# A gated-recurrence layer feeding a cosine-gated MLP in fp32: the start of the kernel reordered, the seven products taken in another order, and the quarter sums of w_out made earlier

## The chip, the cores and the metric

The kernel runs on one core of one Trainium2 chip. The metric is the device time of one execution in microseconds. The kernel before took 660.46 us (the median of three runs: 659.95, 660.46 and 667.34).

## The reference, cut to what matters

Inputs `q, k, v, a_re, a_im` have the shape (B=4, H=8, S=768, D=48); `w_in` is 384 x 2048 and `w_out` 2048 x 384, both in double precision, so that the kernel must turn their 64-bit words into fp32.

```python
mag = np.sqrt(a_re*a_re + a_im*a_im)
scale = np.minimum(mag, 0.999) / (mag + 1e-06)
a_re_n, a_im_n = a_re*scale, a_im*scale
for t in range(S):
    S_re, S_im = (ar*S_re - ai*S_im + k[t] (x) v[t],  ar*S_im + ai*S_re)
    y[t] = q[t] @ S_re
x = y.transpose(0, 2, 1, 3).reshape(B*S, H*D)     # 3072 x 384
h = x @ w_in
out = (h * np.cos(h)) @ w_out                     # 3072 x 384
```

The recurrence is a complex decay for each head and each key dimension; its product over time can be written as exp of a sum of logarithms times a cosine or sine of a sum of angles.

## The kernel before, in words

**Tiling.** The 768 steps of each batch are cut into chunks of 128, which makes 24 chunks (`n`), and two chunks make a group (`g`), 12 groups in all. For a group, the function `log_steps` makes log magnitude and tangent of the half angle from `a_re` and `a_im` on ScalarE and VectorE; for group 0 it runs separately for each of the two halves (`i` = 0, 1; the two generators are called `one` and `two`), each half 128 x 384 elements. `p_powers` sums the logarithms over the steps with a matmul against a triangle of ones (`lgs`, constant tile `sums`) and takes exp of plus and minus the sum (`P`, `Q`). `even_steps` refines them on VectorE. `g_angle` takes the arctangent, `g_phase` sums the angles with another triangle (`phs`, constant tiles `turns` and `last`), `g_trig` takes sine and cosine. `p_apply` and `g_stack` multiply keys and queries by them (`ks`, `qs`), each then of width 96. For groups 0 and 1 TensorE transposes them (`tp`, with `ident`); from group 2 on VectorE's block transpose and a round trip through DRAM does it (`moved`, L922 to L928).

**The chunk.** `f_scores` makes scores (`sc`) and VectorE masks them with `causal` (`atm`); `f_rows` or `f_out` multiplies them by the values and adds queries times the state carried from the chunk before (`yr`, `yp`); `state_sums` and `state_next` carry the state. The state must be multiplied by the decay over the whole chunk: the last row of `P`, moved from one partition to 96 by way of DRAM. `even_steps` issues these DMAs on SyncE's queue: `row` (L828), and, when that has landed, two `end` (L831). VectorE scales `end` in `p_end` (L839) and uses it in `state_next`.

**The MLP.** `mm1_sums` makes h in pieces `hp` (eight for a group), `gate_sine` and `gate_product` make h cos h. For groups 0 and 1 `mm2` multiplies by `w_out` directly (`op`). From group 2 on (`PLAIN`), each pair of chunks is a 2 x 2 block product done as seven products of half size instead of eight (`seventh`, L1150), with sums of blocks on the left (`mixed`, tiles `s`) and on the right (`quarters` and `last_quarter`, tiles `t_s1`, `t_s2`, `t_a22`, and `w_out`'s upper right block overwritten). Four of the seven add into one bank of PSUM that is never cleared between them (`sum`: products 0, 3, 5, 6), three have banks of their own (`op`: 1, 2, 4). ScalarE copies a scaled running sum out (`scalar.mul` into `ot`), VectorE adds an `op` product to it.

**Order.** Each engine runs its instructions in program order. Up to L1543 the order on TensorE, VectorE and ScalarE is written out by hand (L1292 to L1542): groups 0 and 1 with the conversion of the weights, a `piece` being one VectorE step of a weight tile, `lows` the ScalarE step, and 16 raw tiles of 768 KB fetched on GpSimd's queue through four buffers. After that the loop at L1548 weaves for each group n the chunks of n, the MLP products of n-1 and the preparation of n+1, each part given a stretch of the iteration (0 to 1); a scheduler then orders the engines' queues, with some orders fixed by hand (`behind`).

**The start.** SyncE's queue issues the loads of group 0 (`re`, `im` of both halves, then `k`, `q`, then `v`) and of group 1. `constant` (L534) puts a constant's load on ScalarE's queue, and six of them (L575 to L580) stand in the program ahead of ScalarE's first activation table (L1293). GpSimd waits for the second half of `im` by copying one element (`wait_for`, L1283) before it fetches raw weights. `busy(n)` issues n matmuls on a tile of ones, whose results are not used, to keep TensorE occupied.

Of the kernel before, what the change touches and what calls it, by code (L numbers as in the profile page):

```python
# [487 lines left out]
def fast_path(ctx, tc, q, k, v, a_re, a_im, moe_w_in, moe_w_out, out, least, odd, wide,  # L488
# [7 lines left out]
    nc = tc.nc  # L496
# [37 lines left out]
    def constant(array, name, queue=nc.scalar, pool=consts):  # L534
        t = pool.tile(list(array.shape), F32, name=name)
        queue.dma_start(out=t, in_=nc.inline_tensor(array, name=name + "_const").ap())
        return t
# [37 lines left out]
    ident = constant(np.eye(C, dtype=np.float32), "ident", pool=stage["pool"])  # L575
    upto = [constant(sums_np[0], "sums", pool=stage["pool"])]
    turns = [constant(sums_np[0] * np.float32(1.0 / math.pi), "turns", pool=stage["pool"])]
    last = constant(last_np, "last", pool=stage["pool"])
    carry = constant(carry_np, "carry")
    causal = constant(causal_np * np.float32(0.25), "causal")  # L580
# [70 lines left out]

    late = {}
    tail = {}

    def chain(ins, engine="scalar"):

        if engine in tail:
            behind(ins, tail[engine])
        tail[engine] = ins

    def behind(ins, other):
        tc.add_manual_dep(ins.ins, other.ins.name, mybir.DependencyInfo(
            mybir.DependencyClass.NoSync, mybir.DependencyReason.DATA))
# [71 lines left out]
    def log_steps(g, i, n):  # L735
# [10 lines left out]
        chain(nc.scalar.activation(out=m2, in_=re, func=AF.Square))  # L746
        chain(nc.scalar.activation(out=sq, in_=im, func=AF.Square))
# [62 lines left out]
    def even_steps(g, i, n):  # L810


        x = X[g]
        u = cut(x["mag"], i, n)
        P, Q = cut(x["P"], i, n), cut(x["Q"], i, n)
        ins = [vector.scalar_tensor_tensor(out=u, in0=Q, scalar=HUGE, in1=P,
                                           op0=ALU.min, op1=ALU.mult)]
        yield
        for t in P, Q:
            ins.append(vector.scalar_tensor_tensor(out=t, in0=u, scalar=3.0, in1=t,  # L820
                                                   op0=ALU.subtract, op1=ALU.mult))
            yield

        for one_, what in zip(ins, ("carried", "split")):
            if what in x and g > PEG:
                behind(one_, x[what])
        row = x["row"][ds(i * DM, n * DM)]
        nc.sync.dma_start(out=row, in_=P[C - 1:C].rearrange("o x -> (o x)"))  # L828
        end = x["end"][:, ds(i * H, n * H)]
        for a in range(2):  # L830
            nc.sync.dma_start(out=end[ds(a * D, D)], in_=row.rearrange("(x d) -> d x", d=D))  # L831
# [280 lines left out]
    def quarters():  # L1112

        for name in "s1", "s2", "a22":
            right[name] = stage["pool"].tile([C, HJ, E2], F32, name="t_" + name)
        t1, t2, t4 = (right[name] for name in ("s1", "s2", "a22"))
        for j in range(0, HJ, 2):
            for t, a, b in (t1, b12, b11), (t2, b22, t1), (t4, b21, t2):
                yield lambda t=t, a=a, b=b, j=j: behind(vector.tensor_tensor(
                    out=t[:, ds(j, 2)], in0=a[:, ds(j, 2)], in1=b[:, ds(j, 2)],  # L1120
                    op=ALU.subtract), Y[PLAIN * G]["masked"])
# [28 lines left out]
    def seventh(g, p, part):  # L1150
# [19 lines left out]
        if p in (0, 2, 5) or p == 6 and not alone:  # L1170
            late["scalar"] = scalar.mul(out={0: c11, 2: c21, 5: c22, 6: c12}[p], in_=ps, mul=scale)
        if g == NG - 1 and p == 5:
            scalar.mul(out=c12, in_=ps, mul=scale)
        if p in (1, 3, 4, 5) or alone:
            part_ = {1: c11, 3: c21, 4: c21, 5: c22, 6: c12}[p]
            added = vector.scalar_tensor_tensor(out=part_, in0=x["op"] if p == 5 else ps, scalar=scale,
                                                in1=part_, op0=ALU.mult, op1=ALU.add)
            if alone:
                behind(added, late["read DVE"])
            late["vector"] = added  # L1180
# [3 lines left out]
        elif p == 5:  # L1184
# [105 lines left out]
    pieces = [weight(dst, src) for dst, src in parts[:RAW]]  # L1290
# [365 lines left out]
```

## Time and profile before

| | us |
|---|---|
| runs | 659.95, 660.46, 667.34 |
| profiled execution, its own time | 667.46 |
| its span | 665.7 |
| TensorE busy | 650.7 (98%) |
| VectorE busy | 490.6 (74%) |
| ScalarE busy | 393.5 (59%) |
| GpSimd busy | 27.9 (4%) |
| mean granted TensorE clock | 0.988 |

The span runs from the first to the last instruction in the profile; 1.76 us of the execution's own time lie outside it. PE is TensorE's matmuls, PEld its weight loads, DVE is VectorE, ACT ScalarE, POOL GpSimd, SP SyncE; SPq, ACTq and POOLq are the DMA issues of these queues. A line such as `DVE atm L679 [7.87 <-PE sc L690]` says that VectorE stood idle for 7.87 us ahead of this instruction and that the matmuls `sc` ended the wait. Many operations go through a helper that records them all, so that L679 (VectorE and ScalarE), L690 (matmuls) and L710 (activations from a table) say little, and the tile's name says what it is. PEclk is the share of TensorE's full clock that was granted.

### The profile page before, as it was taken

What the parts mean: (1) busy time and instruction counts of PE and PEld (TensorE: products, weight loads), DVE (VectorE), ACT (ScalarE), POOL (GpSimd) and SP (SyncE); (2) the same over time, 40 slices, a digit from 0 to 9 for tenths busy, and PEclk for the clock granted to TensorE, in tenths of its full rate; (3) what the DMA queues carried; (4) which work ended last, traced back from release to release, by engine and by line L of the source; (5) the groups of instructions that cost most, each with busy time, mean ns of one, the idle gap of its engine ahead of it and who ended that gap; (6) DMA issues with size and microseconds to landing.
All of it is one profiled execution on the core that took longest, in us unless ns stands there. A gap on an engine that the chain in (4) does not pass through costs nothing.

```text
span 665.7 us, 10771 instructions
## 1 busy us (share of the span) xinstructions
PE 650.7 (98%) x4077; PEld 582.8 (88%) x4077; DVE 490.6 (74%) x797; ACT 393.5 (59%) x728; POOL 27.9 (4%) x47
## 2 busy tenths in 40 slices
PE   8899999999999999999999999999999999999996
PEld 6797977776899899899899899999999989999896
DVE  4977989869886887876877867876877868862251
ACT  6848696475484485485485485476476476432230
POOL 2011010000000010000000000000000000000000
PEclk9969999999999999999999999999999999999999
DMA  9946684727816827836837746846846853363001
GB/s 242 209 153 149 169 289 77 187 68 148 208 28 130 220 81 159 202 106 152 217 100 162 201 109 135 225 115 132 227 118 132 225 120 96 119 142 96 25 1 31
DMA packets 233626, 94.90 MB, mean 143 GB/s; under 512 B 208846, under 2 KB 222033, under 8 KB 233564
## 3 DMA queue, kind: packets, MB, share of 16 engines
q1 hardware_dynamic: 226924, 68.52, 45.1%
q0 software_dynamic: 5632, 25.17, 11.3%
q8 instruction: 34, 0.56, 0.4%
q10 hardware_dynamic: 1008, 0.43, 0.3%
q14 instruction: 28, 0.23, 0.1%
HBM read 69.28 MB, written 24.81 MB: 141 GB/s over the span
## 4 chain that ended last, share of the span: by engine, by line
PE 79%; DMA 7%; DVE 6%; ACT 2%; SPq 2%; issue 2%; POOL 0%; DVEq 0%; POOLq 0%
PE hp L690 31%; PE op L690 17%; PE sum L690 13%; PE sc L690 5%; PE yp L690 5%; PE sp L690 3%; PE phs L690 2%; DMA qT<-moved 2%; SPq L925 2%; PE lgs L690 1%; DMA raw<-in_moe_w_out_dram 1%; DMA xT<-x 1%; DVE mag L679 1%; PE yr L690 1%; DVE qs L679 1%
## 5 line engine op out<-in xcount | busy, mean ns | idle before, releaser
L690 PE MATMUL hp<-xT,w_in 128*128 128x256 f32 (+1 forms) x1176 | 255.3, 378 | 0.9 <-DMA xT<-x 0.9
L690 PEld LDWEIGHTS hp<-xT,w_in 128*128 128x128 f32 x1176 | 222.2, 193 | 31.9 <-DMA xT<-x 1.4
L710 ACT ACTIVATE gate<-hp,half_pi_b 128x512 f32<-128x512 f32 x96 | 66.0, 687 | 119.5 <-PE hp L690 119.5
L679 DVE TENSOR_TENSOR gate<-hp,gate 128x512 f32<-128x512 f32 x96 | 65.5, 682 | 48.2 <-ACT junk L679 48.1
L690 PE MATMUL op<-w_out,gate 128*128 128x192 f32 (+1 forms) x448 | 100.7, 374 | 0.0
L690 PEld LDWEIGHTS op<-w_out,gate 128*128 128x128 f32 x448 | 75.9, 190 | 16.9 <-issue 2.0
L679 ACT ACTIVATE junk<-hp 128x512 bf16<-128x512 f32 x96 | 56.7, 591 | 0.0
L679 DVE TENSOR_TENSOR atm<-sc,causal 128x512 f32<-128x512 f32 x48 | 32.8, 687 | 31.9 <-PE sc L690 31.9
L690 PE MATMUL sum<-t_s,s 128*128 128x192 f32 x320 | 55.4, 326 | 0.0
L690 PEld LDWEIGHTS sum<-t_s,s 128*128 128x128 f32 x320 | 52.5, 190 | 0.3 <-DVE ot L679 0.3
L679 ACT ACTIVATE ot<-sum 128x192 f32<-128x192 f32 x30 | 9.5, 320 | 70.4 <-PE sum L690 70.4
L690 PEld LDWEIGHTS sc<-qT,kT 96*128 96x128 f32 x384 | 47.5, 192 | 3.4 <-issue 1.2
L690 PE MATMUL sc<-qT,kT 96*128 96x128 f32 x384 | 49.3, 276 | 0.7 <-DMA qT<-moved 0.3
L679 DVE SCALAR_TENSOR_TENSOR ot<-op,ot 128x192 f32<-128x192 f32 x31 | 11.0, 355 | 33.8 <-ACT ot L679 24.8
L690 PE MATMUL yp<-atm,v 128*48 128x128 f32 x352 | 33.6, 277 | 1.1 <-DVE atm L679 1.1
L706 ACT ACT_TABLE_LOAD x24 | 30.8, 1283 | 4.0 <-DMA ident<-ident_const 3.6
L690 PEld LDWEIGHTS sp<-v,ks 128*96 128x96 f32 x320 | 29.7, 165 | 0.0
L690 PE MATMUL sp<-v,ks 128*96 128x48 f32 x320 | 29.7, 245 | 0.0
L690 PE MATMUL yp<-qT,state 96*48 96x128 f32 x304 | 29.6, 272 | 0.0
L690 PE MATMUL sum<-w_out,gate 128*128 128x192 f32 x160 | 29.6, 329 | 0.0
L690 PE MATMUL op<-t_a,gate 128*128 128x192 f32 x160 | 29.0, 332 | 0.0
L679 ACT COPY yT<-yp 48x512 f32<-48x512 f32 x44 | 25.3, 574 | 4.7 <-PE yp L690 4.3
(138 smaller groups left out, 981.9 us busy)
## 6 DMA issues: line engine op xcount, KB each, us to landing
moved<-tr SPq DMA_DIRECT2D x20, 768.0 KB
raw<-in_moe_w_in_dram POOLq DMA_DIRECT2D x16, 768.0 KB, 5.2
raw<-in_moe_w_out_dram POOLq DMA_DIRECT2D x16, 768.0 KB, 4.8
kT<-moved SPq DMA_DIRECT2D x40, 192.0 KB
qT<-moved SPq DMA_DIRECT2D x10, 768.0 KB
k<-in_k_dram SPq DMA_DIRECT2D x24, 192.0 KB
q<-in_q_dram SPq DMA_DIRECT2D x24, 192.0 KB
v<-in_v_dram SPq DMA_DIRECT2D x24, 192.0 KB
```

What stands on the lines that cost most here:

```text
L679: ins = getattr(self.engine, op)(**kw)
L690: chain(nc.tensor.matmul(out, **kw), "tensor")
L706: chain(nc.scalar.preload_act_table_set(table))
L710: chain(nc.scalar.activation(func=func, **kw))
L925: nc.sync.dma_start(out=X[g][name][:, ds(i * H, n * H), q4], in_=moved[q4])
```

## The change

It has five parts. (1) The helper `constant` now puts its load on GpSimd's queue by default, in a fixed order, and the six constants move: `sums`, `turns`, `last`, `ident` directly after GpSimd's wait, which is now for `re` instead of `im`; `causal` between the second and third raw weight tile; `carry` after the fourth. ScalarE's first instruction is then the table load. (2) In group 0 the squares of the second half are done on VectorE, the steps of the two halves are interleaved in another order, and the filler matmuls are 25, then 6 and 10, instead of 33, then 10. (3) The `row` and `end` transfers of group 0 go out on ScalarE's queue, once for both halves, `row` ahead of the first sine and `end` behind the second half's cosine. The values of group 1 are loaded after its keys and queries instead of before everything else of group 1. (4) The seven products are taken in the order 0, 1, 3, 2, 5, 4, 6, with the evictions changed to suit, and for the last iteration of the loop two products instead of three are placed in the first part. (5) All twelve instructions of `quarters` stand ahead of the loop instead of in the iteration of group 2, and are no longer held behind that group's masks.

```diff
-    def constant(array, name, queue=nc.scalar, pool=consts):
+    def constant(array, name, queue=None, pool=consts):
         t = pool.tile(list(array.shape), F32, name=name)
-        queue.dma_start(out=t, in_=nc.inline_tensor(array, name=name + "_const").ap())
+        put = (queue or nc.gpsimd).dma_start(
+            out=t, in_=nc.inline_tensor(array, name=name + "_const").ap())
+        if queue is None:
+            chain(put, "gpsimd")
...
-    ident = constant(np.eye(C, dtype=np.float32), "ident", pool=stage["pool"])
-    upto = [constant(sums_np[0], "sums", pool=stage["pool"])]
-    turns = [constant(sums_np[0] * np.float32(1.0 / math.pi), "turns", pool=stage["pool"])]
-    last = constant(last_np, "last", pool=stage["pool"])
-    carry = constant(carry_np, "carry")
-    causal = constant(causal_np * np.float32(0.25), "causal")
...
-        chain(nc.scalar.activation(out=m2, in_=re, func=AF.Square))
-        chain(nc.scalar.activation(out=sq, in_=im, func=AF.Square))
+        for out_, in_ in (m2, re), (sq, im):
+            if g == 0 and i > 0:
+                if in_ is im:
+                    yield
+                vector.tensor_tensor(out=out_, in0=in_, in1=in_, op=ALU.mult)
+            else:
+                chain(nc.scalar.activation(out=out_, in_=in_, func=AF.Square))
...
-        row = x["row"][ds(i * DM, n * DM)]
-        nc.sync.dma_start(out=row, in_=P[C - 1:C].rearrange("o x -> (o x)"))
-        end = x["end"][:, ds(i * H, n * H)]
+        if g > 0:
+            row_out(g, i, n, nc.sync)
+            row_back(g, i, n, nc.sync)
+
+    def row_out(g, i, n, queue):
+        P = cut(X[g]["P"], i, n)
+        queue.dma_start(out=X[g]["row"][ds(i * DM, n * DM)],
+                        in_=P[C - 1:C].rearrange("o x -> (o x)"))
+
+    def row_back(g, i, n, queue):
+        row = X[g]["row"][ds(i * DM, n * DM)]
+        end = X[g]["end"][:, ds(i * H, n * H)]
         for a in range(2):
-            nc.sync.dma_start(out=end[ds(a * D, D)], in_=row.rearrange("(x d) -> d x", d=D))
+            queue.dma_start(out=end[ds(a * D, D)], in_=row.rearrange("(x d) -> d x", d=D))
...
         for j in range(0, HJ, 2):
             for t, a, b in (t1, b12, b11), (t2, b22, t1), (t4, b21, t2):
-                yield lambda t=t, a=a, b=b, j=j: behind(vector.tensor_tensor(
-                    out=t[:, ds(j, 2)], in0=a[:, ds(j, 2)], in1=b[:, ds(j, 2)],
-                    op=ALU.subtract), Y[PLAIN * G]["masked"])
+                vector.tensor_tensor(out=t[:, ds(j, 2)], in0=a[:, ds(j, 2)],
+                                     in1=b[:, ds(j, 2)], op=ALU.subtract)
...
-        if p in (0, 2, 5) or p == 6 and not alone:
-            late["scalar"] = scalar.mul(out={0: c11, 2: c21, 5: c22, 6: c12}[p], in_=ps, mul=scale)
+        if p in (0, 3, 5) or p == 6 and not alone:
+            late["scalar"] = scalar.mul(out={0: c11, 3: c21, 5: c22, 6: c12}[p], in_=ps, mul=scale)
...
-        if p in (1, 3, 4, 5) or alone:
-            part_ = {1: c11, 3: c21, 4: c21, 5: c22, 6: c12}[p]
-            added = vector.scalar_tensor_tensor(out=part_, in0=x["op"] if p == 5 else ps, scalar=scale,
+        for part_ in {1: [c11], 2: [c21], 4: [c21, c22], 6: [c12] * alone}.get(p, []):
+            added = vector.scalar_tensor_tensor(out=part_, in0=ps, scalar=scale,
...
-        elif p == 5:
+        elif p == 4:
...
-                for p in range(lo, hi) for part in range(2)]
+                for p in (0, 1, 3, 2, 5, 4, 6)[lo:hi] for part in range(2)]
...
-    load(1, ("v",))
     after = consts.tile([1, 1], F32, name="after")
-    wait_for(X[0]["im"][0:1, G - 1, 0, 0:1])
-    load(1, ("re", "im", "k", "q"))
+    wait_for(X[0]["re"][0:1, G - 1, 0, 0:1])
+    upto = [constant(sums_np[0], "sums", pool=stage["pool"])]
+    turns = [constant(sums_np[0] * np.float32(1.0 / math.pi), "turns", pool=stage["pool"])]
+    last = constant(last_np, "last", pool=stage["pool"])
+    ident = constant(np.eye(C, dtype=np.float32), "ident", pool=stage["pool"])
+    load(1, ("re", "im", "k", "q", "v"))
...
-    pieces = [weight(dst, src) for dst, src in parts[:RAW]]
+    pieces = [weight(dst, src) for dst, src in parts[:2]]
+    causal = constant(causal_np * np.float32(0.25), "causal")
+    pieces += [weight(dst, src) for dst, src in parts[2:RAW]]
+    carry = constant(carry_np, "carry")
...
-    busy(33)
+    busy(25)
     one, two = (log_steps(0, i, 1) for i in range(2))
-    for _ in range(5):
-        next(one), next(two)
+    for steps in one, two, one, one, two, one, one, two, one, two, two, one, two, one:
+        next(steps)
     for i in range(2):
         p_powers(0, i)
-    busy(10)
+        busy(6 + 4 * i)
     for _ in range(3):
-        next(one), next(two)
+        next(two)
     g_angle(0, 0, 2)
...
     next(two, None)
+    row_out(0, 0, G, scalar)
     g_trig(0, 0, 1)
     p_apply(0, 0, 1)
     g_phase(0, 1)
     g_trig(0, 1, 1)
+    row_back(0, 0, G, scalar)
     busy(10)
...
+    quarters()
     for n in range(2, NG):
         weave((mixes(n - 1, 2, 4), 0.0, 0.12), (logs(n + 1), 0.0, 0.02), (chunks(n), 0.0, 0.36),
-              (upper[2:] if n == 2 else [], 0.0, 0.2), (products(n - 1, 0, 3), 0.0, 0.36),
+              (upper[2:] if n == 2 else [], 0.0, 0.2), (products(n - 1, 0, 2 + (n < NG - 1)), 0.0, 0.36),
               (prods(n + 1), 0.25, 0.27), (second(n - 1, 1), 0.36, 0.5),
-              (products(n - 1, 3, 7), 0.4, 0.56),
+              (products(n - 1, 2 + (n < NG - 1), 7), 0.4, 0.56),
...
-              (quarters() if n == PLAIN else [], 0.4, 0.9),
```

More of the change, by code (lines that the diff above doesn't have):

```diff
@@ L532, in fast_path, with chain, behind @@
     carry_np = np.where(step_np == C - 1, np.float32(math.pi), np.float32(0.0))[:, None]
-    def constant(array, name, queue=nc.scalar, pool=consts):
+    late = {}
+    tail = {}
+    def chain(ins, engine="scalar"):
+        if engine in tail:
+            behind(ins, tail[engine])
+        tail[engine] = ins
+    def behind(ins, other):
+        tc.add_manual_dep(ins.ins, other.ins.name, mybir.DependencyInfo(
+            mybir.DependencyClass.NoSync, mybir.DependencyReason.DATA))
+    def constant(array, name, queue=None, pool=consts):
         t = pool.tile(list(array.shape), F32, name=name)
-        queue.dma_start(out=t, in_=nc.inline_tensor(array, name=name + "_const").ap())
+        put = (queue or nc.gpsimd).dma_start(
+            out=t, in_=nc.inline_tensor(array, name=name + "_const").ap())
+        if queue is None:
+            chain(put, "gpsimd")
         return t
@@ L648, in fast_path @@
     out_scale = 2.0 if moe_w_out.dtype != F32 else 1.0
[L652 to L663, printed above, removed]
     def in_turn(**kw):
```

## The prediction

> **What bounds the kernel now.** I read the page first, then windows of three us over the start, the chain of waits over the first 70 us, and the timeline around each place that the change touches.
>
> ```profile
> span 665.7 us, 10771 instructions
> PE 650.7 (98%) x4077; PEld 582.8 (88%) x4077; DVE 490.6 (74%) x797; ACT 393.5 (59%) x728; POOL 27.9 (4%) x47
> PEclk9969999999999999999999999999999999999999
> ```
>
> TensorE is occupied for all but 15 us. A change can win in the start, where TensorE runs fillers and waits for group 0's preparation; in those few idle us; and in the clock, whose third digit, near 40 us, is 6. The windows (TensorE, weight loads, VectorE, ScalarE, GpSimd, clock, DMA share, GB/s) show that place:
>
> ```profile
> 33.00:36.00 3.00, 3.00 (x33) 3.00 (x33) 1.15 (x2) 2.96 (x5) 0.00 (x0) 1.00 0.85 266
> 36.00:39.00 3.00, 1.71 (x13) 1.59 (x12) 2.12 (x6) 1.90 (x4) 0.00 (x0) 0.88 0.01 0
> 39.00:42.00 3.00, 3.00 (x16) 3.00 (x16) 3.00 (x5) 2.97 (x4) 1.03 (x1) 0.50 0.03 5
> 48.00:51.00 3.00, 3.00 (x12) 2.39 (x12) 0.00 (x0) 0.48 (x1) 0.00 (x0) 0.50 1.12 308
> 51.00:54.00 3.00, 3.00 (x21) 2.51 (x20) 0.85 (x1) 2.60 (x5) 0.00 (x0) 0.85 0.64 113
> ```
>
> From 39 to 51 us half the clock is granted. Lost: 3 x 0.12 + 12 x 0.5 + 3 x 0.15 = 6.8 us, which is the distance of the run of 667.34 from those of 659.95 and 660.46. So I take the profiled execution (667.46 us) for one with the drop and the other two for ones without: 667.46 - 6.8 = 660.7, beside the median of 660.46.
>
> The chain of waits (start, us, what) over the start:
>
> ```profile
> 0.74 2.96 DMA re<-in_a_re_dram
> 3.72 3.92 DMA im<-in_a_im_dram
> ...
> 30.15 1.95 SPq L831
> 32.15 4.67 DMA end<-row
> ...
> 37.14 0.56 DVE state L679
> 37.74 2.76 PE yr L690 x14
> ```
>
> Two waits on DMAs stand in it: the second half of `im` until 7.64, and `end`, 6.7 us from its issue to its landing at 36.82, for which VectorE idles 2.69 us and TensorE 1.3. In between, ScalarE and VectorE work on group 0 without a pause. Four lines of the timeline more:
>
> ```profile
> 3.58 1.28 ACT L706 ACT_TABLE_LOAD   x1 [3.58 <-DMA ident<-ident_const]
> 12.31 0.91 PE L690 MATMUL lgs<-lg,sums 128*128 128x384 f32 x2 [0.25 <-DVE lg L679]
> 137.76 0.69 DVE L679 TENSOR_TENSOR atm<-sc,causal 128x512 f32<-128x512 f32 x1 [7.87 <-PE sc L690]
> 150.54 0.42 PE L690 MATMUL yp<-atm,v 128*48 128x128 f32 x4 [0.77 <-DVE atm L679]
> ```
>
> The table waits behind six DMA issues; the first real matmul comes at 12.31; VectorE has a hole of 7.87 us shortly before TensorE waits for it.
>
> **What the Trainium skill says.** "TensorE: Matmul & The Clock Gate", Part 1: the clock is either half or full, decided over a free-running window of about 3.4 us, so that the same kernel varies from run to run. The trace agrees on the two levels (1.00 and 0.50; 0.88 and 0.85 hold a transition); that it stayed low for 12 us with TensorE occupied the page doesn't explain. "DMA: Bandwidth & Descriptors", Issuing engines are not separate DMA queues: DMAs from any engine share 16 DMA engines, another queue saves only issue time. Agrees: the constants' queue took 3.4% of those engines over the first 40 us, 1.36 us, beside the loads. "ScalarE: Activation LUTs", What ACT_TABLE_LOAD costs: 1283 ns and a drain of 1380; here 1.28 us, and the square follows 0.02 us after it, so with nothing ahead of it I count no drain.
>
> **Part 1, table and constants.** Removed from ScalarE: six issues of 0.40 to 0.45 us, up to 3.56. The table now runs from about 0.75 to 2.0, ahead of any data. The loads lose a rival worth 1.36 us of DMA time. I take 0.4 of it for the first half of `re` (landing 3.3 instead of 3.70), and all for the second halves: `re` 5.3 instead of 6.66, `im` 6.3 instead of 7.64. The new issues on GpSimd: a wait until 5.3, a copy of 0.17, four issues of 0.79 (as the raw tiles', 3.15 for four), the first out at 6.3. No row shows a 64 KB load from GpSimd; the DMA page's Bandwidth and Latency sections give about 1 us to the first byte and 0.95 for 64 KB, so `sums` lands at 8.3; at worst it takes the 8.2 us of a contended raw tile and lands at 14.5. I take 8.5, because little else is in flight but k and q. Raw tiles 0 to 3 start some 2 us later than at 8.06; they are first used at 26.22, so it costs nothing; were they not there by 23, each us late would cost one.
>
> **Part 2, the two halves.** ScalarE and VectorE both loaded, I follow the new order with the durations shown (activation 0.43 to 0.52 apart, VectorE 0.47 to 0.55, the 768-wide arctangent 0.84). First squares end at 4.7, sum at 5.2, Ln and two Exp at 6.7; VectorE squares `re` meanwhile (0.56 in place of 0.52 on ScalarE). Two VectorE steps end at 7.1, the second `im` square and sum at 8.2, the log difference of half 0 at 8.7 (before: 12.25). The 25 fillers end at about 9.1 (4, 9 and 12 in the first three windows of three us), so `lgs` runs at 9.2 and `sums` has just landed. Half 1's `lgs` follows at 10.8 (13.78), the arctangent at 14.0 (16.93), the last of the six refinement steps at 15.8 (19.6), the first phase at 16.0 (19.54). From there to 34.1 both orders hold the same work on a VectorE that never pauses: 3.5 us earlier throughout. Bounds: 1.5, if `sums` is 2 us late, and 4.
>
> **Part 3, powers' ends.** On ScalarE one `row` issue (0.24 us) goes into a hole (it idled 0.36 ahead of that sine) and two `end` issues (1.5 us for both, as SP's at 157.28) behind the second cosine; queued behind them are the copies of `kT`, which had waited 1.00 for TensorE, so 0.5 us is lost and I give up 0.3 of part 2. `row` to landing was 2.8 us, the two sines and the cast between span 3: no wait. `end` issued at 20 and landing by 25 is far ahead of its use at 34.14 - 3.5 = 30.6. So VectorE's 2.69 us go; state at 31.5 instead of 37.70. What is late next: TensorE's own queue (`yr` of chunk 1 stood ready at 36.13, now 32.6; 1.6 us of its wait go), then ScalarE, full from 30 to 36, whose chain log, exp, table, arctangent of group 1 comes next. I count 1.3 us at that arctangent, the idle time of TensorE. Values of group 1 later: first read near 74, loaded by 35; cost nothing, and they leave SP's queue, which one issue of four loads held for 13.02 us. Parts 1 to 3: 3.5 - 0.3 + 1.3 = 4.5 us; bounds 1 and 6. From 57 us on TensorE has no waits worth naming until 137, so the gain should carry; VectorE, full from 57 to 84, moves with it.
>
> **Part 4, products.** Same matmuls, same eight evictions. TensorE waits for a running sum's eviction once:
>
> ```profile
> 617.45 2.87 PE L690 MATMUL sum<-w_out,s 128*128 128x192 f32 x16 [0.42 <-ACT ot L679]
> ...
> 621.22 4.15 PE L690 MATMUL hp<-xT,w_in 128*128 128x256 f32 x18 [0.90 <-DMA xT<-x]
> ```
>
> The 0.42 alone would be given back to the 0.90 behind it. With one product (2.6 us) moved behind the last chunk, `yp` and `xT` come up to 2.6 us earlier, and both waits go: 1.3 us, unless the copies of `yp` stay behind ScalarE's guard of a raw tile, which ended at 608.29: then 0. I take 0.6.
>
> **Part 5, quarter sums.** Twelve of 0.47 us, 5.6, fit into the 7.87 us hole, since the last weight step ends at 129. VectorE is then 5.6 us less loaded from 141 to 161, and the two waits of `yp` for masks (0.77 and 0.29) go: 1.0 us, between 0 and 1.1. If they landed after 137.76 instead, masks would wait: up to 1 us lost.
>
> **Sum:** 660.7 - 4.5 - 0.6 - 1.0 = 654.6; beside the median of 660.46, 654.4. I say 654.5.
>
> **Rivals.** (A) *The drop stays.* Its stretch has the same small matmuls (48 and 128 columns), only the idle 1.3 us are gone. For it: TensorE stayed slow while fully occupied. Against: two of three runs escaped even with the idle time. If the median has it: 654.5 + 6.8 = 661.3. (B) *Hidden anyway:* the earlier start meets a chain that doesn't move (ScalarE from 30 to 36, raw tiles by DMA), and only 1 us of 4.5 arrives: 658. (C) *Slower:* constants from GpSimd's queue land late behind k, q and raw tiles on full DMA engines (share 1.0 to 1.2 from 3 to 21 us). `sums` at 14.5 would make `lgs` 2.2 us later than before; removed waits (1.3, 1.0 and 0.6) still outweigh it. From 15.2 us on (12.3 + 2.9) it decides; at 18, 2.8 us lost: 663.3. Against: 64 KB each, issued ahead of the raw tiles.
>
> **How the numbers follow.** Chances: forecast 0.57 (651.5 to 656.5), A 0.17, B 0.18 (656.5 to 660), C 0.08. An interval from 651.5 to 661.3 holds the forecast, B and half of A, 0.83. A measurement of this kernel tells some 2% (13 us) from no change; 647 needs more than all bounds together (6 + 1.3 + 1.1 = 8.4), unless the runs before are of the 667 kind; 673.7 needs the drop and C. Faster 0.03, same 0.95, slower 0.02.
>
> **What would show it.** Table load below 1 us; `lgs` near 9.2 with `busy` its only predecessor; arctangent of group 0 near 14; no VectorE wait for `end`, state near 31.5; clock 1.00 from 33 to 54; `t_s` between 130 and 137, no `yp` wait near 150; no `sum` wait near 610. Wrong would make me: a TensorE wait on `sums`, `turns` or `ident`, a ScalarE pause before `end`, or the low clock again.

## The result, and the profile after

The changed kernel takes 657.8 us (median of 22 runs, 655.6 to 660.31). The kernel before, measured in turn with it on the same chip, takes 661.07 (22 runs, 657.56 to 669.0). The ratio is 0.9941, with an interval of 0.9921 to 0.9961: about 4 us less, a small gain that the interval keeps apart from nothing. The profiled execution of the changed kernel took 657.8 us, its span 656.0.

From the page of the kernel after:

```profile
span 656.0 us, 10759 instructions
PE 641.3 (98%) x4075; PEld 575.7 (88%) x4075; DVE 492.4 (75%) x799; ACT 392.5 (60%) x726; POOL 32.0 (5%) x53
PEclk9999999999999999999999999999999999999999
```

The 6 in the clock's row is gone, and TensorE's busy time is 9.4 us less; some 6.8 of them are the half speed that is gone. The windows that showed the drop before (same columns):

```profile
36.00:39.00 3.00, 3.00 (x30) 3.00 (x29) 2.94 (x5) 2.93 (x5) 0.76 (x1) 1.00 0.02 5
39.00:42.00 3.00, 3.00 (x30) 3.00 (x29) 3.00 (x4) 2.24 (x3) 0.00 (x0) 1.00 0.83 252
```

From 36 to 39 TensorE is now busy for 3.00 us instead of 1.71, and from 39 to 42 it does 30 matmuls in place of 16. Now the start, from the timelines (start, duration, engine, instruction, and in brackets the idle time ahead of it and what ended it). Before:

```profile
16.93 0.84 ACT L710 ACTIVATE tan<-tan 128x768 f32<-128x768 f32 x1
...
23.56 1.08 PE L937 MATMUL tp<-ident,ks 128*96 128x128 f32 x8 [0.22 <-DVE ks L679]
24.23 1.07 ACT L679 COPY kT<-tp 96x512 f32<-96x512 f32 x2 [1.00 <-PE tp L937]
25.90 2.05 PE L690 MATMUL sc<-qT,kT 96*128 96x128 f32 x16 [0.24 <-ACT qT L679]
...
37.74 0.42 PE L690 MATMUL yr<-state,qT 96*128 96x48 f32 x2 [1.29 <-DVE state L679]
```

After:

```profile
0.74 1.28 ACT L703 ACT_TABLE_LOAD   x1 [0.74 <-PEq L1657]
9.48 0.88 PE L687 MATMUL lgs<-lg,sums 128*128 128x384 f32 x2 [0.69 <-DMA sums<-sums_const]
...
14.93 0.84 ACT L707 ACTIVATE tan<-tan 128x768 f32<-128x768 f32 x1
...
16.95 0.49 ACTq L676 DMA_DIRECT2D row<-lg  x1
...
20.38 0.60 ACT L707 ACTIVATE rs<-rs,half_pi_b 128x384 f32<-128x384 f32 x1
22.93 1.02 ACTq L676 DMA_DIRECT2D end<-row  x2
24.00 1.07 ACT L676 COPY kT<-tp 96x512 f32<-96x512 f32 x2 [3.01 <-DMA v<-in_v_dram]
...
25.60 2.05 PE L687 MATMUL sc<-qT,kT 96*128 96x128 f32 x16 [2.28 <-ACT qT L676]
...
34.03 0.55 DVE L676 SCALAR_TENSOR_TENSOR state<-sp,end 96x384 f32<-96x384 f32 x1
```

Down to the last cosine, which ends at 20.98, everything is some 2.3 us earlier than before (TensorE's `tp` at 21.30, before 23.56). Then ScalarE stands still for 3.01 us: the next instruction in its queue is the issue of the two `end` transfers, which read what `row` wrote and so have to wait until it has landed, and behind it stand the copies of `kT` and `qT` that TensorE needs. The first scores start at 25.60, and 25.90 was their time before: nearly the whole lead is gone. The profile names the values' transfer as what ended the wait; that it is the `end` issue that waited is read from its place, 22.93, just ahead of the copy, and tested below (ends behind the copies). The chain of waits (start, us, what) goes back the same way:

```profile
10.88 12.75 DMA v<-in_v_dram
...
24.00 1.07 ACT kT L676 x2
...
25.60 2.05 PE sc L687 x16
```

In place of the chain of before, which went through `end` to the state at 37.14, it now goes through loads of group 1's data into ScalarE's copies, 13 us ahead of that. The state comes without a wait of VectorE, at 34.03 instead of 37.14.

Three landmarks show where the two profiled executions come apart. The phase of group 1 (`phs`) starts at 47.12 instead of 55.33: 8.2 us, of which 6.8 are the clock. From the start of group 2's `hp` (156.39, before 164.41) to the one at 563.68 (571.46), eight groups take 407.3 us after and 407.1 before: no gain. The last group's pitch, `hp` to `hp`, is 48.07 us instead of 49.76: 1.7. With 0.2 in the tail that is 8.0 - 0.2 + 1.7 + 0.2 = 9.7, the whole difference of the spans (665.7 and 656.0).

At the quarter sums and the masks of the next chunk (timeline after):

```profile
126.27 1.02 DVE L676 TENSOR_TENSOR t_a<-w_out,t_s 128x384 f32<-128x384 f32 x2
129.52 0.69 DVE L676 TENSOR_TENSOR atm<-sc,causal 128x512 f32<-128x512 f32 x1 [2.23 <-PE sc L687]
...
142.02 0.43 PE L687 MATMUL yp<-atm,v 128*48 128x128 f32 x4 [0.59 <-ACT Q L707]
143.40 0.43 PE L687 MATMUL yp<-atm,v 128*48 128x128 f32 x4 [0.29 <-DVE atm L676]
```

The sums lie in VectorE's hole, which shrank from 7.87 to 2.23 us, yet TensorE waits at the same two places: 0.59 for ScalarE's `Q` where it had been 0.77 for a mask, and 0.29 as before.

One way of reading the runs is used below. Every run comes with its mean granted clock. Time multiplied by that clock is the time it would have taken at full clock, and the rest is what the lowered clock cost (the clock is given to 0.001, so a single run is known to 0.3 us). An idle TensorE at a low clock is counted as lost too, and there is some of that at the very end: in 13 of the 14 profiles the clock falls once more behind the last matmul, while the output is written. That makes 0 to 1.5 us of "lost" which cost no time, 0.7 on average; in the changed kernel's profile it is all there is (from 653 us on). So only differences between kernels count, and a "lost" of 0.7 is as good as none.

### The profile page after: what moved, and what is told of

The parts are those of the page before. It is cut to its first block, busy times and chain, and to the rows that moved or that the text cites. A ratio compares the mean times of both kernels' runs of the same rounds, so it can differ in the third digit from the quotient of the medians.

```text
span 656.0 us, 10759 instructions
## 1 busy us (share of the span) xinstructions
PE 641.3 (98%) x4075; PEld 575.7 (88%) x4075; DVE 492.4 (75%) x799; ACT 392.5 (60%) x726; POOL 32.0 (5%) x53
## 4 chain that ended last, share of the span: by engine, by line
PE 86%; DMA 6%; SPq 2%; DVE 2%; ACT 2%; issue 1%; ACTq 0%; DVEq 0%
PE hp L687 34%; PE op L687 16%; PE sum L687 15%; PE sc L687 6%; PE yp L687 6%; PE sp L687 4%; DMA v<-in_v_dram 2%; PE phs L687 2%; SPq L584 1%; DMA xT<-x 1%; PE lgs L687 1%; DMA qT<-moved 1%; DMA x<-yT 1%; PE yr L687 1%; SPq L936 1%
## 5 line engine op out<-in xcount | busy, mean ns | idle before, releaser
L687 PE MATMUL hp<-xT,w_in 128*128 128x256 f32 (+1 forms) x1176 | 252.7, 376 | 1.0 <-DMA xT<-x 1.0
L687 PEld LDWEIGHTS hp<-xT,w_in 128*128 128x128 f32 x1176 | 219.9, 190 | 31.5 <-DMA xT<-x 0.9
L676 ACT ACTIVATE ot<-sum 128x192 f32<-128x192 f32 x40 | 12.8, 322 | 52.8 <-PE sum L687 52.6
L676 DVE SCALAR_TENSOR_TENSOR ot<-op,ot 128x192 f32<-128x192 f32 x41 | 13.6, 353 | 39.5 <-PE op L687 37.9
L676 ACT CAST tan<-phs 128x384 int32<-128x384 f32 x24 | 11.4, 482 | 29.4 <-PE phs L687 29.4
```

The source lines that it names most:

```text
L676: ins = getattr(self.engine, op)(**kw)
L687: chain(nc.tensor.matmul(out, **kw), "tensor")
```

## Experiments

Each ratio is to the kernel before as measured beside that variant, with its 95% interval. "At full clock" is the median of time times clock, "lost" the mean of the rest. The kernel before was measured anew beside four sets of variants: 661.4 us at full clock (beside changed again, ends behind copies, values held, ends on SyncE), 660.3 (before with fillers, before with ends, old split, old quarters), 661.0 (values held and ends behind, changed with fillers, old order) and 660.8 (before with order), with 2.2, 2.2, 2.3 and 2.5 lost. Figures from different sets are compared through these.

| | median, us (runs) | ratio | at full clock | lost |
|---|---|---|---|---|
| changed, first time | 657.8 (22) | 0.9941 [0.9921, 0.9961] | 656.0 | 1.7 |
| changed, again | 658.85 (22) | 0.9931 [0.9905, 0.9956] | 657.1 | 1.8 |
| ends behind copies | 657.28 (10) | 0.9914 [0.9872, 0.9956] | 657.2 | 1.1 |
| values held | 656.45 (11) | 0.9897 [0.9869, 0.9926] | 656.0 | 0.7 |
| ends on SyncE | 663.75 (22) | 1.0016 [0.9993, 1.0039] | 657.8 | 6.0 |
| before, fillers | 661.62 (23) | 0.9986 [0.9966, 1.0006] | 660.9 | 1.0 |
| before, ends | 660.49 (22) | 0.9982 [0.9962, 1.0002] | 659.7 | 1.0 |
| old split | 658.17 (22) | 0.9948 [0.9927, 0.9969] | 656.0 | 2.0 |
| old quarters | 658.56 (22) | 0.9944 [0.9919, 0.9968] | 656.5 | 2.0 |
| values held, ends behind | 656.59 (11) | 0.9907 [0.9879, 0.9935] | 655.5 | 0.7 |
| changed, fillers | 658.81 (22) | 0.9958 [0.9939, 0.9976] | 657.9 | 0.8 |
| old order | 661.16 (14) | 0.9985 [0.9959, 1.0012] | 658.7 | 2.5 |
| before, order | 659.27 (22) | 0.9972 [0.9945, 0.9999] | 658.2 | 2.2 |

My theory after the first result was: ScalarE's stop at the `end` issue eats the start's gain; most of the rest is the clock. The rivals: another chain holds the start up (TensorE's queue or ScalarE from 30 to 36), or the gain of the start was never there.

**The changed kernel again**, to see what a repetition does.

> The changed kernel once more, as the yardstick for its variants on the same chip: 655.6 to 660.3 us, some 3 us under the kernel before. The pause of ScalarE ahead of kT's copies (3.0 us) and TensorE's wait for qT (2.3 us) should be there again.

Measured 658.85. The wait of the first scores is 1.82 us this time, the group-1 phase at 46.71; other waits fall elsewhere (1.34 us at an `hp` at 461, 1.02 at the scores at 533). So waits of 1 us for transfers come and go between executions, and one profile's sum is good to some 1 or 2 us. ScalarE's `end` issue comes 5.3 us after `row`'s here, 6.0 in the first profile, and 5.3 to 6.1 in the four other kernels below with the same start (old split, old quarters, changed with fillers, old order).

**Ends behind the copies.** The issue moves in ScalarE's queue behind the first two copies:

```diff
     g_trig(0, 1, 1)
-    row_back(0, 0, G, scalar)
     busy(10)
...
     turn(0, 0)
+    row_back(0, 0, G, scalar)
```

> The two transfers of the powers' ends are issued on ScalarE's queue behind the copies of kT and qT of the first chunk instead of ahead of them; nothing else is moved. Theory (ScalarE's queue stands still until the row has landed): the scores of chunk 0 begin near 23.3 us instead of 25.6, TensorE's wait of 2.3 us goes, and the kernel is about 2 us faster than the changed one. Rival (the copies wait for something else that lands at 23.6, such as the values): the scores stay at 25.6 and the time at the changed kernel's.

Measured 657.28, 1.6 less than the changed kernel beside it (10 runs only, interval wide; one of them took 664.76 at a clock of 0.990). From its timeline:

```profile
23.69 0.34 ACTq L676 DMA_DIRECT2D end<-row  x1
...
23.87 2.05 PE L687 MATMUL sc<-qT,kT 96*128 96x128 f32 x16 [0.27 <-ACT qT L676]
```

The `end` issues stand behind the first copies, the stop is gone, the scores start 1.7 us earlier than in the changed kernel, and the phase of group 1 comes at 45.78 instead of 47.12 and 46.71. So the theory of the stop holds for the start. The 2 us of time that it forecast aren't shown: 657.2 at full clock against 657.1. At the end of the profiled execution nothing of it is left (span 657.0, as the repetition's): 1.50 us are lost at an `hp` at 88.04, where TensorE waits for ScalarE's `hi`, and 0.9 at two `hp` that wait for `xT`.

**Values held.** The diff says that group 1's values are loaded last, but the changed kernel's trace shows all four `v` loads at 7.28, ahead of group 1's `im`: the scheduler brought them forward, since nothing held them. Here they are tied behind the last load of `q`:

```diff
-    load(1, ("re", "im", "k", "q", "v"))
+    load(1, ("re", "im", "k", "q"), put=noting)
+    load(1, ("v",), put=held)      # held: behind the last of those
```

> The values of group 1 are really held behind the keys and queries of group 1 on SyncE's queue; in the changed kernel the scheduler has put them back in front. Rival theory (the DMA engines are full of values and raw weights, which makes row land 6 us after its issue): row lands 2 to 3 us earlier, ScalarE pauses under 1 us, 2 us faster than the changed kernel. Theory (the order on ScalarE's queue): row still needs about 2.8 us from its issue at 17.0, so that a pause of under 1 us would be left; then both hold and it is the transfer's length that decides. If the pause stays at 3 us, the values have no part in it.

Measured 656.45, ratio 0.9897, 2.4 us under the changed kernel beside it; about 1 of them is clock. From its timeline:

```profile
21.58 0.91 ACTq L676 DMA_DIRECT2D end<-row  x2
...
24.14 2.05 PE L687 MATMUL sc<-qT,kT 96*128 96x128 f32 x16 [0.81 <-ACT qT L676]
```

With two loads of 192 KB less in front, `row` is back 1.35 us earlier (4.6 us from its issue at 16.96 to that of `end`, instead of 6.0, or 5.3 in the repetition) and the wait shrinks from 2.28 to 0.81. So these loads make up a part of the stop, 0.7 to 1.35 us. The time came out as expected, but `row` was to be 2 to 3 us earlier, and what holds `row` for the other 4.6 us isn't shown: the DMA engines were at a share of 1.04 to 1.22 from 15 to 27 us in the changed kernel, and at 1.04 to 1.39 here.

**Ends on SyncE**, all else as changed:

```diff
-        if g > 0:
-            row_out(g, i, n, nc.sync)
-            row_back(g, i, n, nc.sync)
+        row_out(g, i, n, nc.sync)
+        row_back(g, i, n, nc.sync)
...
-    row_out(0, 0, G, scalar)
...
-    row_back(0, 0, G, scalar)
```

> The row and end transfers go out on SyncE's queue as before, all else as changed (the shorter start, quarter sums, products). Theory: ScalarE has no pause, the scores of chunk 0 begin near 23.3 us; but row stands behind the loads of im and re on SyncE's queue, end lands near 34 us, and VectorE waits for it as before, 2 to 3 us with TensorE idle some 1 us: the time is within 1.5 us of the changed kernel. If the ends on ScalarE's queue were worth what was forecast, it is 3 us slower and the drop of the clock comes back in some runs.

Measured 663.75, ratio 1.0016: the whole gain is gone. That is 4.9 us slower than the changed kernel beside it, not "within 1.5 us"; the last sentence, against my theory, came true and more. Its waits and windows:

```profile
37.96 0.66 PE L687 MATMUL yr<-state,qT 96*128 96x48 f32 x2 [3.74 <-DVE state L676]
```

```profile
36.00:39.00 3.00, 1.04 (x5) 1.04 (x6) 1.91 (x5) 0.20 (x1) 0.00 (x0) 0.73 0.00 0
39.00:42.00 3.00, 3.00 (x16) 3.00 (x16) 3.00 (x5) 2.97 (x4) 1.04 (x1) 0.50 0.00 0
```

The scores start at 23.66, with no stop, but VectorE gets `end` at 37.06, no earlier than before, so that the lead turns into a longer wait for the state: 3.74 us instead of 1.29. The longer wait lowers the clock more often: 6.0 us lost on average, and 19 of 22 runs below 0.995 (its 657.8 at full clock is too low by up to half of the 3.74 idle us). The earlier start without the ends costs more in clock than it brings, though the order's gain is in this kernel too.

**The kernel before with fillers**, for the clock alone. Six matmuls on the tile of ones stand where TensorE waits for the state:

```diff
     f_columns(0)
+    busy(6)
```

> The kernel before with six filler matmuls (1.3 us, results unused) put where TensorE waits for the first state; nothing else. Theory (that idle time is what lets the clock drop): granted clock 0.998 or more, no run far above the lowest, the median some 1.5 to 3 us under the kernel before, with no other gain. Rival (the stretch of small matmuls drops the clock by itself): the clock is as low as before in a good part of the runs and the median is as before or 1 us above.

Measured 661.62, ratio 0.9986. Neither side came out whole: the drop became rare, as the theory said, but the median didn't fall, as the rival said. Lost on average 1.0 us instead of 2.2: one run of 23 had a mean clock below 0.995, against 14 of the 75 of before. But it is 0.6 slower at full clock, and the one low run, which is the profiled one, still shows 0.50 from 42 to 48 us behind a wait of 0.68 that the fillers left. Occupying TensorE makes the drop rarer and costs about what it saves in the median.

**The kernel before with the ends alone** (rows on ScalarE's queue as in the change, with `row_out` and `row_back` called at the same places, nothing else).

> The kernel before with one thing of the change: the powers' ends on ScalarE's queue, once for both halves. Theory (the ends are the whole gain, the shorter start gives none of its own): the wait for the state and the clock's drop go; ScalarE pauses for row as in the changed kernel, 1 to 2 us; the time is within 1.5 us of the changed kernel. Rival (the ends need the earlier start to pay): half of the gain at most, ratio 0.996 or above.

Measured 660.49, ratio 0.9982; none of 22 runs had a clock below 0.995. There is no wait for the state in its profile and no stop: `row` goes out at 19.28, 2.3 us later than in the changed kernel, `end` at 22.93, right behind the second cosine (22.73), and the copies wait for TensorE as before (0.99). So here `row` had landed when `end` came to be issued, 3.65 us after it went out at the latest; the same transfer on the same queue took 5.3 to 6.0 us with the earlier start. That the two `end` issues both stand at 22.93 is chance; whether the landing itself moved isn't shown. The ends alone take away the drop (about 1.2 us on average) and 0.7 us at full clock: 1.65 us in the mean, which the interval of the ratio doesn't keep apart from nothing. That is the rival's "half of the gain at most".

**Old split**: three of the seven products in the first part for the last group too.

```diff
-              ... (products(n - 1, 0, 2 + (n < NG - 1)), 0.0, 0.36),
+              ... (products(n - 1, 0, 3), 0.0, 0.36),
...
-              (products(n - 1, 2 + (n < NG - 1), 7), 0.4, 0.56),
+              (products(n - 1, 3, 7), 0.4, 0.56),
```

> The changed kernel with three products instead of two in the first part of the loop's last iteration, as before; the new order of the products stays. Theory (the split alone brings the 1.3 us seen near 610): TensorE waits 0.9 us or more for xT ahead of the last group's hp, 1 us slower than the changed kernel. Rival (the order brings it, since no product adds to the bank that was just read): no wait, same time.

Measured 658.17, as the changed kernel. The last group's pitch is 48.00 us and neither wait is there, so the split that I had given the gain to isn't needed: the rival holds.

**Old quarters**: the quarter sums again in the iteration of group 2, behind its masks.

```diff
-                vector.tensor_tensor(out=t[:, ds(j, 2)], in0=a[:, ds(j, 2)],
-                                     in1=b[:, ds(j, 2)], op=ALU.subtract)
+                yield lambda t=t, a=a, b=b, j=j: behind(vector.tensor_tensor(
+                    out=t[:, ds(j, 2)], in0=a[:, ds(j, 2)], in1=b[:, ds(j, 2)],
+                    op=ALU.subtract), Y[PLAIN * G]["masked"])
...
-    quarters()
...
+              (quarters() if n == PLAIN else [], 0.4, 0.9),
```

> The changed kernel with the quarter sums back in the iteration of group 2. Theory (a wait for the powers of group 3, 0.59 us, took the place of the wait for the masks, 0.77): 0.2 us slower at most, not to be measured. The forecast's own figure would be 1.0 us slower.

Measured 658.56, ratio 0.9944: no difference to the changed kernel. The wait of `yp` reads 0.76 for a mask again instead of 0.59 for `Q`. Its profile shows something else, in the start:

```profile
25.86 3.22 PE L687 MATMUL sc<-qT,kT 96*128 96x128 f32 x16 [2.13 <-ACT qT L676]
```

```profile
24.00:27.00 3.00, 1.14 (x8) 1.15 (x9) 1.87 (x4) 2.75 (x5) 0.00 (x0) 0.92 1.21 172
27.00:30.00 3.00, 3.00 (x16) 2.94 (x16) 1.57 (x3) 1.08 (x3) 0.29 (x1) 0.51 1.25 206
```

Behind the wait for `qT` (2.13 us) the clock falls to one half for some 3 us (3 x 0.08 + 3 x 0.49 = 1.7 us lost), and 16 matmuls run in the window from 27 to 30, where the changed kernel's has 32. The start in this kernel is that of the change. So the change moves the drop rather than ending it: the wait for the state is gone, the wait for the first scores is new and can lower the clock too, for a shorter time. Of the five profiles with this start and a wait of 1.80 to 2.28 us there, two show the drop.

**Values held and ends behind the copies**, both edits of above together.

> Both repairs of the start together on the changed kernel: the values of group 1 held behind its keys and queries, and the ends issued behind the copies of kT and qT. Theory (ScalarE's pause for row is what eats the earlier start, and the idle TensorE behind it sometimes loses the clock): scores of chunk 0 near 23.5 us, no wait of TensorE above 0.5 us before 45, median 656.0 or less, 2 to 3 us under the changed kernel, the kernel to keep. Rival (what is won at the start is lost at a later wait for a DMA): 657 to 658.

Measured 656.59, ratio 0.9907. The scores wait 0.27, the phase of group 1 starts at 45.22, 0.7 us are lost. The median lies between what the theory (656.0 or less) and the rival (657 to 658) had said. At full clock it is the lowest, 655.5, but the interval of its ratio overlaps that of "values held", and an `hp` at 459.75 waits 1.68 for `xT`. Either is about 1 to 2 us under the changed kernel.

**The changed kernel with fillers** ahead of the first scores:

```diff
+    busy(10)
     f_scores(0, 0)
```

> The changed kernel with ten filler matmuls (2.2 us, results unused) where TensorE waits for qT ahead of the first scores. Theory (the new idle time of 1.8 to 2.3 us drops the clock for some 3 us in part of the runs, as one profile showed, and makes the runs of 659 to 661): these runs become rare, the lowest stay at 656, the median falls by about 1 us to 657. Rival (the spread comes from the DMAs' landing times near 155, 460 and 533): spread and median as in the changed kernel.

Measured 658.81, ratio 0.9958: 0.8 us lost instead of 1.7 or 1.8, no run of 22 at a clock of 0.995 or below, against 7 of the 44 of the changed kernel, but the scores only at 26.74, and no gain in the median. It fits the wait for the scores costing the changed kernel 1 us of clock on average, and fillers are no cure.

**Old order** of the seven products (0 to 6, with the old evictions) in the changed kernel:

```diff
-                for p in (0, 1, 3, 2, 5, 4, 6)[lo:hi] for part in range(2)]
+                for p in range(lo, hi) for part in range(2)]
```

> The changed kernel with the old order of the seven products and the old evictions; the new split (two products instead of three in the first part of the last iteration) stays. Theory (the order is what removes the wait for the bank just read and the wait for xT behind it): the 0.42 us wait is back ahead of the seventh product near 610 and 0.5 to 1 us is lost there; within 1 us of the changed kernel, not told apart by time. Rival (the split alone is enough): no wait near 610.

Measured 661.16, ratio 0.9985: some 2 us of the gain went with the order (at full clock 2.3 us are left of 4.3), more than expected. Its timeline:

```profile
457.59 2.87 PE L687 MATMUL sum<-t_s,s 128*128 128x192 f32 x16 [1.44 <-DVE ot L676]
...
612.84 2.87 PE L687 MATMUL sum<-w_out,s 128*128 128x192 f32 x16 [0.42 <-ACT ot L676]
```

The 0.42 of the kernel before is back; the wait of 0.90 behind it isn't, so the new split alone took that one, and the last group's pitch, 48.76, lies between the two. At 457 a product waits 1.44 us until VectorE has read the running sum's bank, and VectorE had stood before that at a raw weight tile that had not landed (3.25 us). This wait isn't in the three other profiles with the old order. In the old order product 3 is added from that bank by VectorE; in the new one only ScalarE reads it.

**The kernel before with the order** (order, evictions and split as in the change, nothing else).

> The kernel before with only the seven products' new order: products and evictions alternate sum and op in turn as in the change, with its split; start, ends, quarter sums and values as before. Theory: the order alone takes the waits out of a group, because the bank of the running sum is no longer read by VectorE at a time when VectorE stands at a guard; expected no wait of TensorE at the sum near 457 or near 612 us, 1.3 to 1.7 us less in the last group, a ratio of 0.995 to 0.998 to the kernel before, and still a lowered clock after the state's wait in a good part of the runs, since the start is unchanged. Rival: the waits of the old order in the run with it were chance, or the order pays only with the changed start; expected a ratio of 0.998 to 1.001 with waits of the same length elsewhere.

Measured 659.27, ratio 0.9972 [0.9945, 0.9999]. From its timeline, `sum` and `hp` of the last group without an entry in brackets:

```profile
610.20 2.76 PE L690 MATMUL sum<-w_out,s 128*128 128x192 f32 x16
612.80 20.88 PE L690 MATMUL hp<-xT,w_in 128*128 128x256 f32 x96
```

The pitch is 48.07 us, 1.7 less than before, and 2.5 are gained at full clock. The rival (a ratio of 0.998 to 1.001) isn't shut out by the interval, but the wait of 0.42 at this sum is in all four profiles with the old order (before, before with fillers, before with ends, old order) and in none of the ten with the new one. With the old order and the old split a wait for `xT` follows it, of 0.90, 1.45 and 1.89. The clock is untouched, as expected: 2.2 us lost, before 2.5, and 5 of 22 runs below 0.995.

Its start is that of the kernel before, and yet its profile shows neither the wait for the state nor the drop:

```profile
33.81 0.16 DVE L679 TENSOR_SCALAR end<-end 96x16 f32<-96x16 f32 x1
34.10 0.55 DVE L679 SCALAR_TENSOR_TENSOR state<-sp,end 96x384 f32<-96x384 f32 x1
...
47.15 0.91 PE L690 MATMUL phs<-tan,turns 128*128 128x384 f32 x2 [0.56 <-ACT tan L710]
```

The second `end` went out at 29.09 instead of 30.15 and was there when VectorE came to it. So the old start's wait for the state comes in some executions only, and without it the old start reaches the phase of group 1 at 47.15, where the changed kernel stands at 46.71 or 47.12.

## Why the prediction was right, and where it was not

The time, 657.8, lies within the range of 651.5 to 661.3, but not in the forecast's own range (651.5 to 656.5). It lies in that of rival B, "hidden anyway, and only 1 us of 4.5 arrives". The range is wide enough to hold an unchanged kernel as well (660.46 was the median before), so that it was met says little. And that the whole came within 3.3 us of 654.5 is in part luck: start, ends and quarter sums brought some 3.5 us less than forecast, the order of the products 1.5 to 2 more. Two of the signs named as "Wrong would make me" did appear: TensorE waits for `sums` (0.69 us) and ScalarE pauses before `end` (3.01). The forecast's sum, step by step:

*The base, 660.7 at full clock.* Right to within 1 us: measured later, the kernel before has 660.3 to 661.4. Reading the low stretch as 6.8 us, and the profiled execution as one with the drop, holds.

*Table and constants.* As said: the table load at 0.74 to 2.02 and `lgs` at 9.48 (said 9.2). `sums` is the last to come, by 0.69 us; it landed 3.2 us after its issue at 6.27, where the forecast's estimate (about 1 us and 0.95) had 2, and the three constants behind it took 3.3 to 4.2. The loads gained less than the 0.4 us said: the first square starts at 3.64. Rival C, at 14.5 us or later, had nothing to it.

*The two halves.* Somewhat too much: arctangent at 14.93 (said 14.0), the first phase subtracted at 17.29 (16.0; before 19.54). That is 2.3 us of lead instead of 3.5. From `lgs`, 0.3 late, to the arctangent ScalarE doesn't stop; it has some 0.6 us more to do in that stretch than I had counted.

*Powers' ends: the step that failed.* I wrote that "`row` to landing was 2.8 us, the two sines and the cast between span 3: no wait". The 2.8 us came from another moment: SyncE's `row` of one half (1.5 KB instead of 3.0) at 23.17, with the DMA engines at a share of 0.79 from 21 to 24 us and 1.10 from 24 to 27. The queue and the size aren't what counts, since the kernel before with the ends has the same 3.0 KB on ScalarE's queue back within 3.65 us. Here the `end` issue came 6.0 us after that of `row`, and ScalarE stood for 3.01 of them, with the copies that TensorE needed behind it. I had named these copies and given 0.3 us for them. The cost was 2.0 us at the scores (25.60, against 23.66 and 23.87 in the kernels without the stop). The Trainium skill, which I had cited ("DMA: Bandwidth & Descriptors", Issuing engines are not separate DMA queues), says that all DMAs interleave on the same 16 engines; I used it for the constants and not for `row`. That sharing is the whole cause isn't shown: with two loads less in front 4.6 us remain. And "Values of group 1 later" I took from the diff's text, where the trace after shows them at 7.28. Holding them returned 1.35 us of the 6.0.

*Parts 1 to 3, 4.5 us.* Measured 1.4 at the phase of group 1 (48.5 without the drop, now 47.12), and that is about the wait for the state; against an execution of the old start that was spared this wait (47.15) it is 0 to 0.5. So what the start wins, the stop takes, and what is left is that the wait for the state is in none of the nine profiles with the new start and the ends on ScalarE's queue. Of all but the order, with the new split in it, 2.3 us are left at full clock (old order, 658.7 to 661.0). Without the stop it is 3.3 at the same landmark (45.22), 1.5 to 1.9 us ahead of the changed kernel, of which about 1 reached the end (655.5 at full clock, changed 656.0 and 657.1). Where the rest goes isn't settled: in those profiles waits of 0.5 to 1.7 us on `xT`, `qT` and `hi` appear later, but such waits also come and go in unchanged repetitions.

*Products, 0.6 us.* Too little, and for the wrong reason. Two waits and the spacing around them gave 1.7 in the profiles; at full clock the order gives 2.0 (4.3 for the changed kernel again, less the 2.3 without it) to 2.5 (with the split, on the kernel before), each to within about 1 us. Where more than 1.7 should come from isn't located. "The 0.42 alone would be given back to the 0.90" and "With one product (2.6 us) moved behind the last chunk, `yp` and `xT` come up to 2.6 us earlier, and both waits go" put the gain on the split. The runs show the order: with the old split both waits are gone too, with the old order the wait at the sum stays. The split alone takes away only the wait on `xT`. In the old order products 5 and 6 follow each other and both add into the running sum's bank, so that 6 waits until ScalarE has copied out what 5 left; in the new order an `op` product, with a bank of its own, stands between any two of the four.

*Quarter sums, 1.0 us.* In place as said (121.59 to 127.3), but worth nothing: where the mask no longer was late, ScalarE's `Q` was, 0.59 us, and old quarters made no measurable difference. I had looked at what ended the wait and not at what would have ended it next.

*Rival A, the drop.* In the profile it is gone, and the wait that brought it with it. In the runs it is not all gone: 1.7 to 1.8 us lost on average against 2.2, most likely by the new wait for the scores: with values held, where it is 0.81 or 0.27 us, 0.7 are lost, which the end of the kernel accounts for.

So the gain, 4.0 us in the median and 4.6 in the mean of the repetition, is about 2 to 2.5 from the order of the products, some 2 from start and ends together, and half a us from the clock; the last two are less than they could be because the ends stop ScalarE. The order is shown twice, by taking it out and by putting it in alone. The 2 us of start and ends are what is left over: they show at full clock (2.3 us with old order, to within about 1), but the ratio of old order (0.9959 to 1.0012) doesn't keep them apart from nothing.

## What to carry to other kernels

An instruction that waits for a DMA, put on a compute engine's in-order queue, stops everything behind it (3.01 us here); the same transfer was back within 3.65 us at one moment and after 6.0 at another, so its time to land has to be taken from the moment at which it will run, and what stands behind it must be able to wait. A lead gained at the start is worth only as much as the next thing that doesn't move with it: follow the new order to the first instruction whose releaser is a transfer. Whether a load really comes later is seen from its place in the trace, since a scheduler may bring it forward.

## What the runs showed of the hardware

The clock fell behind short waits of TensorE: 2.13 us in the kernel with old quarters, 1.80 in the one with the old order (0.89 and 0.54 in the windows from 24 to 30 us), 1.29 in the kernel before, 0.68 with fillers in it; a wait of 2.28 in the changed kernel's profile left it at 1.00. So the length of a wait doesn't decide it. The Trainium skill ("TensorE: Matmul & The Clock Gate", What's actually happening) gives the half clock as what follows an idle window of about 3.4 us, and lets this window run freely. The first isn't what is seen here, since these waits are all shorter than such a window, and the measurement decides. The second agrees: the same wait does or doesn't bring the drop, and the time spent at half clock, added up over slices of 0.25 us, is 3.41 us with old quarters, 3.42 with the old order, 6.83 with the ends on SyncE (behind 3.74 us of waiting), 10.24 in the kernel before with fillers and 13.65 in the kernel before, which is 1, 1, 2, 3 and 4 times 3.41. So each further window at half clock costs 1.7 us. Why the drop lasts four windows in one case, with TensorE occupied, and one in another, no run here settles.
